# A new order for the first two batches of a fused attention and MLP kernel: v by heads, the first weight quarter in four parts, batch 1's loads held back

## The chip, the cores and the metric

The kernel runs on one core of a Trainium2 chip. The metric is the device time of one execution in microseconds (us), lower is better. Three runs of the kernel before took 324.17, 324.43 and 324.71 us; the median is 324.43. The profile is of one further execution, taken by the hardware profiler.

The engines are named as the profile names them. PE is TensorE, and PEld its weight loads. DVE is VectorE, ACT is ScalarE, POOL is GpSimd, and SP is SyncE, which here only issues DMAs.

## The reference: what is computed

There are two stages. The first is attention with a sliding window of 128 and a linear bias per head; the second is a two-layer MLP on its output.

```python
scores = scale * np.matmul(q, k.transpose(0, 1, 3, 2))      # 8 batches, 8 heads, 576 x 576, d = 64
mask = (rel >= 0) & (rel < window)                          # rel = query - key, window = 128
scores = np.where(mask, scores + bias[None], -1000000000.0) # bias = -slope[h] * |rel|
attn = softmax(scores); attn_out = attn @ v
x = attn_out.transpose(0, 2, 1, 3).reshape(4608, 512)
h = x @ w_in                                                # 512 -> 2048
g = h * np.clip(h + 3.0, 0.0, 6.0) / 6.0
out = g @ w_out                                             # 2048 -> 512
```

Inputs and output are float32; matmuls run in bf16.

## The kernel before, in words

**Attention** goes by pairs of heads: pair g is batch g // 4, heads 2(g % 4) and the next, 32 pairs in all. A query block of 128 needs only the key block on the diagonal and the one before it. For each pair PE computes the transposed scores into two PSUM tiles, `scd` (diagonal blocks, `scores_diag`) and `sco` (the blocks off it, `scores_off`). ACT takes the exponentials into bf16 tiles `pd` and `po`; in batches 1 and later POOL masks with a select (`exp_diag`, `exp_off`). In batch 0 both tiles, and in batch 1 `sco`, get bias and mask from a table that PE adds by a matmul with the identity (`tables_diag`, `tables_off`). Then PE multiplies by v, which has a column of ones so that the sum of the softmax comes along (`attend` into one tile of the score pool, `attend_split` into two half tiles of other pools, `values` in later batches). DVE takes the reciprocal and multiplies ("norm" of the pair, into `avs`, two buffers). `back` turns the result over into `xT`, by PE and a copy on ACT (on DVE for pairs 7 and part of 3) or, for most pairs from 8 on, by a transposing DMA.

**q and k** arrive in float32, are cast to bf16 (`prepare`, `prepare_double`), turned over on PE and copied to `qTb` and `kTb` (`transposes`, `double_begin` with `double_copy`, `wide_double` through a tile of the score pool, `double`). **v** arrives in token blocks of 128 (`load_block`, 256 KB each, in pieces of 256 bytes) and is cast into `vbuf` (`cast_v`, `cast_tokens`).

**The MLP** goes by blocks `nt` of 512 tokens, nine in all. An up unit U(nt, ms) is four matmuls of 512 columns into one bank `hps`, one per quarter `ks` of the model width, that is per pair of the batch; then ACT takes a relu (L516) and DVE a multiply (L517), which frees the bank. A down unit D is four of the sixteen matmuls (L547) of 128 tokens; after the fourth unit DVE copies the row out (L556). Unit U(0, ms) with ms from 4g to 4g + 3 needs column quarter g of `w_in`. The first quarter comes as plain float32 into `raw`, which lies in `gbuf[0]`, and is cast on chip (`load_raw`, `cast_raw`); the other three are casting DMAs that POOL issues (`load_w_in`), and so is `w_out` in four parts (`load_w_out`). `w_out`'s buffer holds batch 0's `pd` and `po` before, and `gbuf[1]` those of batch 1.

**Order.** The order on every engine is the order of the program (manual scheduling); an engine that waits holds all that stands behind it. `units` lists all U and D, by the strings in `ORDER`; `fill(n)` emits the next n units, but stops at a U whose tokens are not yet finished (`done`). `first_batch` and `second_batch` write the first two batches out by hand, then `segment` runs pairs 8 to 31, with `FILLS` units at fixed places of each pair.

**PSUM.** There are eight banks: two tiles of two banks for scores ("sc"), one "av", two "h", one "o". `hps` takes "h"; for nt = 0 `UP_BANKS` sends units 2, 8, 12 to "av" and 5, 11 to "o". A down row takes "o", except the first of nt = 1 and two of the last block.

**Queues.** SP issues nearly all loads, in order; ACT issues the first k loads and one v block. Plain DMAs share eight completion semaphores in turn, so that one can be issued only when the one eight before it has landed. POOL's casting DMAs stand in POOL's own order among its casts and selects.

The lines that the change and the prediction touch: `load_block` L108, `memsets` L140 and `memsets_later` L144, `load_raw` L176, `cast_raw` L179, `second_w_in` L187, `cast_v` L191, `prepare_double` L235, `wide_double` L276, `exp_diag` L371, `attend_split` L444, `back` L462, `up_begin` L496, `ORDER` L559, `first_batch` L604, `second_batch` L679, `FILLS` L741.

Of the kernel before, what the change touches and what calls it, by code (L numbers as in the profile page):

```python
# [10 lines left out]
FP32 = mybir.dt.float32  # L11
# [7 lines left out]
def kernel(  # L19
# [120 lines left out]
    def memsets():  # L140
        nc.gpsimd.memset(vbuf[0][:, :, :, D:W], 1.0)
        nc.gpsimd.memset(vbuf[0][64:128, 4, :, 0:D], 0.0)

    def memsets_later():  # L144
        for i in range(2):
            nc.gpsimd.memset(p4buf[i], 1.0)
        nc.gpsimd.memset(kTb[1][:, :, 4, LAST:128], 0.0)
        nc.gpsimd.memset(vbuf[1][:, :, :, D:W], 1.0)
        nc.gpsimd.memset(vbuf[1][64:128, 4, :, 0:D], 0.0)
        nc.gpsimd.memset(tbuf[64:128, :, 4, :], 0.0)  # L150
# [310 lines left out]

    def back(g, tag=None):  # L462
        b, hp = divmod(g, NP)
# [6 lines left out]
        tag = tag or ("o" if b < 2 else "h")  # L470
        tp = BANKS[tag].tile([128, SP], BF16, tag=tag, name="tb", padded_shape=[128, 1024])
        for j in range(NQ):
# [22 lines left out]

    def up_begin(nt, ms, n):  # L496
        hps = ps_h.tile([128, NT], FP32, tag="h", name="hps")
        up_mms(nt, ms, 0, n, hps)
        begun[nt, ms] = hps, n
# [34 lines left out]
    def moe_down(nt, step):  # L534
# [14 lines left out]
        if part == 3:  # L549
# [36 lines left out]
    def stage_next(g):  # L586
# [14 lines left out]
        if VCAST.get(g):  # L601
            cast_tokens(VCAST[g], "v")

    def first_batch():  # L604
        prepare(0, (V, A))
        load_block(0, "v", 1, nc.scalar)
        for j in (4, 0, 2, 3):
            load_block(0, "v", j, nc.sync)
        load_raw()
        warm_up(5)  # L610
        tables_diag(0)
        tables_off(0)
# [12 lines left out]
        exp_full(1)  # L625
        double_copy(0, 1, "q", 0, (V, V))
        double_copy(0, 1, "k", 0, (A, A))
        scores_diag(2)
        double_copy(0, 1, "q", 1, (V, V))
        double_copy(0, 1, "k", 1, (V, V))  # L630
        tables_off(2)
        scores_off(2)
        exp_full(2)
        scores_diag(3)
        cast_v(0, 4, P)
        cast_v(0, 0, P)
        cast_v(0, 1, P)
        cast_v(0, 2, V)
        cast_v(0, 3, V)
        scores_off(3)  # L640
        exp_full(3)
        attend(0)
        for dp in range(2):
            for nm in "kq":
                load_double(1, dp, nm, nc.sync)
        load_tokens(1, "v")
        attend_split(1, ("av", "h"))
        attend(2)
        back(0, "o")
        cast_raw(0, P)  # L650
        cast_raw(1, P)
        attend(3)
        cast_raw(2, A)
        back(1, "av")
        cast_raw(3, P)
        prepare_double(1, 0, (P,), "k")
        second_w_in()
        up_begin(0, 0, 1)
        up_begin(0, 1, 1)
        back(2, "o")  # L660
        prepare_double(1, 0, (V,), "q")
        up_more(0, 0, 2)
        up_more(0, 1, 2)
        back(3, "av")
        wide_double(1, 0, "k", V)
        wide_double(1, 0, "q", A)
        up_more(0, 0, 3)
        up_more(0, 1, 3)
        done[0] = NP
        fill(2)  # L670
        prepare_double(1, 1, (P,), "k")
        load_w_in(2)
        prepare_double(1, 1, (P,), "q")
        load_w_in(3)
        for dp in range(2):
            for nm in "kq":
                load_double(2, dp, nm, nc.sync)

    def second_batch():  # L679
        scores_diag(NP + 0)  # L680
        exp_diag(NP + 0, 0)
        exp_diag(NP + 0, 1)
        fill(2)
        scores_off(NP + 0)
        exp_off_full(NP + 0)
        wide_double(1, 1, "k", V)
        fill(1)
        wide_double(1, 1, "q", V)
        fill(1)
        scores_diag(NP + 1)  # L690
        exp_diag(NP + 1, 0)
        exp_diag(NP + 1, 1)
        fill(2)
        scores_off(NP + 1)
        exp_off_full(NP + 1)
        fill(1)
        cast_tokens(1, "v")
        scores_diag(NP + 2)
        exp_diag(NP + 2, 0)
        exp_diag(NP + 2, 1)  # L700
        fill(1)
        scores_off(NP + 2)
        exp_off_full(NP + 2)
        fill(2)
        for i in range(0, 4):
            load_w_out(i)
        g = 2 * NP - 1
        scores(g)
        exp_diag(g, 0)
        exp_diag(g, 1)  # L710
        prepare_double(2, 0, (V, P))
        prepare_double(2, 1, (P, P))
# [5 lines left out]
        exp_off_full(g)  # L718
        fill(1)
        attend(NP)  # L720
        fill(1)
        attend(NP + 1)
        fill(1)
        back(NP)
        attend(NP + 2)
        fill(1)
        back(NP + 1)
        double(2, 0, "k", 0, "av", A)
        attend(NP + 3)
        back(NP + 2)  # L730
        double(2, 0, "k", 1, "av", A)
        wide_double(2, 0, "q", A)
        up_begin(1, 0, 3)
        back(2 * NP - 1)
        up_begin(1, 1, 3)
        done[0] = 2 * NP
        fill(2)
# [52 lines left out]
    with tc.manual_schedule(engines=every):  # L790
# [7 lines left out]
        memsets()  # L798
        memsets_later()
        first_batch()  # L800
        second_batch()
        fill(2)
        segment(2 * NP, G, lambda g: FILLS.get(g, (1, 1, 1, 2, 0, 1, 2)))
# [32 lines left out]
```

## Time and profile before

| | us |
|---|---|
| device time, median of three (lowest, highest) | 324.43 (324.17, 324.71) |
| profiled execution: first to last instruction (span) | 321.8 |
| PE busy in the span | 308.2 (96%) |
| ACT, DVE, POOL busy | 196.0, 175.5, 138.4 |
| bytes moved by DMA | 52.43 MB, 118977 of 131426 packets under 512 B |
| one matmul of 512 columns, start to start, at full clock | 0.216 |
| one up or down unit of four such | 0.865 |

The profiler gives the span and not a device time of its own for that execution; 324.43 less 321.8 leaves 2.6 us around the span.

How to read it: a line of the timeline has the start, the length, the engine, the line of the code, the operation, output and input tiles and their shape, and how many instructions were merged; in brackets stands how long the engine sat idle before it and what it waited for. In the chain of waits each line is a start, a length and what the time went to. The end of a matmul is modelled, so a busy PE can still wait: where it matters, starts are compared.

### The profile page before, as it was taken

The numbers are of one execution on the slowest core, as the hardware profiler recorded it, in microseconds if no ns is written. First come the engines' busy times: TensorE is split into PE (matmuls) and PEld (weight loads), VectorE is DVE, ScalarE is ACT, GpSimd is POOL, SyncE is SP. The second block draws the span as 40 slices with busy tenths as digits, with TensorE's granted clock in tenths as the row PEclk, the third lists the DMA queues.
The fourth block names the chain that finished last, engine by engine and source line by source line (L and its number), as shares of the span: only waits on it lengthen the run. The fifth ranks groups of instructions, "written<-read, shape, count | busy, mean of one in ns | idle before, by whom it ended". The sixth has DMA issues, their size and how long they took to land.

```text
span 321.8 us, 6865 instructions
## 1 busy us (share of the span) xinstructions
PE 308.2 (96%) x2620; PEld 164.6 (51%) x2659; DVE 175.5 (55%) x346; ACT 196.0 (61%) x337; POOL 138.4 (43%) x247
## 2 busy tenths in 40 slices
PE   6888999999999999999999999999999999999996
PEld 3564465455555545455667655455454444444443
DVE  6686595564346655555555556554655455445510
ACT  3857977877777766766676667666764344244401
POOL 7364590665494767446654663663331000000000
PEclk9999999999999999999999999999999999999999
DMA  7999999899999999999799999922011200000112
GB/s 273 262 369 210 269 233 214 235 200 189 201 256 170 242 200 189 204 202 230 179 214 207 211 189 202 236 66 89 20 55 59 80 34 34 33 33 35 65 49 83
DMA packets 131426, 52.43 MB, mean 163 GB/s; under 512 B 118977, under 2 KB 122817, under 8 KB 131393
## 3 DMA queue, kind: packets, MB, share of 16 engines
q1 hardware_dynamic: 125648, 46.15, 67.0%
q0 software_dynamic: 3696, 3.67, 7.0%
q10 hardware_dynamic: 2048, 2.16, 2.2%
q8 instruction: 21, 0.34, 0.5%
q14 instruction: 13, 0.10, 0.1%
HBM read 36.70 MB, written 9.44 MB: 143 GB/s over the span
## 4 chain that ended last, share of the span: by engine, by line
PE 83%; DMA 7%; ACT 4%; issue 2%; DVE 2%; POOL 1%; SPq 0%; ACTq 0%; DVEq 0%
PE ops L547 37%; PE hps L492 35%; DMA gbuf<-in_moe_w_in_dram 3%; PE scd L324 2%; DMA w_in_sb<-in_moe_w_in_dram 2%; PE av L419 2%; DMA ldbuf<-in_k_dram 2%; PE av L411 2%; ACT r L516 2%; PE sco L356 1%; PE ops L528 1%; DVE gbuf L517 1%; PE tp L254 1%; ACT gbuf L379 1%; ACT xT L479 1%
## 5 line engine op out<-in xcount | busy, mean ns | idle before, releaser
L517 DVE SCALAR_TENSOR_TENSOR gbuf<-r,hps 128x512 bf16<-128x512 f32 x144 | 98.5, 687 | 102.3 <-ACT r L516 99.4
L516 ACT ACTIVATE r<-hps,bias 128x512 f32<-128x512 f32 x144 | 98.8, 690 | 90.4 <-PE hps L492 89.3
L492 PE MATMUL hps<-xT,w_in_sb 128*128 128x512 bf16 (+1 forms) x622 | 143.3, 357 | 2.3 <-DMA w_in_sb<-in_moe_w_in_dram 0.9
L547 PE MATMUL ops<-w_out_sb,gbuf 128*128 128x512 bf16 x539 | 134.0, 379 | 2.4 <-issue 1.7
L492 PEld LDWEIGHTS <-w_in_sb 128*128 128x128 bf16 x640 | 59.0, 98 | 55.3 <-issue 1.7
L547 PEld LDWEIGHTS <-gbuf 128*128 128x128 bf16 x560 | 52.2, 98 | 56.9
L382 POOL TENSOR_SCALAR_AFFINE_SELECT pd<-pd 128x512 bf16<-128x512 bf16 x48 | 29.5, 631 | 37.8 <-ACT pd L379 37.7
L392 POOL TENSOR_SCALAR_AFFINE_SELECT po<-po 128x512 bf16<-128x512 bf16 x48 | 30.1, 633 | 32.6 <-ACT po L389 32.4
L556 DVE COPY osb<-ops 128x512 f32<-128x512 f32 x33 | 22.7, 688 | 22.0 <-PE ops L547 21.9
L379 ACT ACTIVATE pd<-scd,bias_d 128x512 bf16<-128x512 f32 x48 | 31.5, 684 | 4.7 <-PE scd L324 4.7
L389 ACT ACTIVATE po<-sco,bias_o 128x512 bf16<-128x512 f32 x48 | 33.1, 690 | 0.0
L206 POOL CAST tbuf<-ldbuf 128x512 bf16<-128x512 f32 (+1 forms) x45 | 25.5, 611 | 17.1 <-issue 17.1
L430 DVE TENSOR_TENSOR avs<-av,rc 128x384 bf16<-128x384 f32 (+1 forms) x48 | 23.6, 491 | 1.6
L419 PEld LDWEIGHTS <-pd 128*128 128x128 bf16 x192 | 14.3, 97 | 7.9 <-issue 0.5
L411 PE MATMUL av<-vbuf,po 128*128 128x65 bf16 x192 | 18.0, 193 | 0.0
L419 PE MATMUL av<-vbuf,pd 128*128 128x65 bf16 x192 | 17.3, 194 | 0.0
L411 PEld LDWEIGHTS <-po 128*128 128x128 bf16 x192 | 14.3, 98 | 2.9 <-DVE avs L430 0.5
L395 ACT ACTIVATE p4buf<-sco,bias_d 128x64 bf16<-128x64 f32 x48 | 15.6, 325 | 0.0
L199 POOL CAST vbuf<-ldbuf 128x1024 bf16<-128x1024 f32 x14 | 14.2, 1041 | 2.4 <-DMA ldbuf<-in_v_dram 2.4
L324 PEld LDWEIGHTS <-kTb 64*128 64x128 bf16 x256 | 7.3, 94 | 14.3 <-issue 10.0
L324 PE MATMUL scd<-qTb,kTb 64*128 64x128 bf16 x256 | 12.7, 219 | 1.9 <-ACT kTb L232 1.2
L239 POOL CAST pr<-ldbuf 128x576 bf16<-128x576 f32 x18 | 11.5, 671 | 2.0 <-DMA ldbuf<-in_k_dram 1.9
(107 smaller groups left out, 216.7 us busy)
## 6 DMA issues: line engine op xcount, KB each, us to landing
out_dram<-osb SPq DMA_DIRECT2D x33, 256.0 KB, 2.5
ldbuf<-in_v_dram SPq DMA_DIRECT2D x31, 256.0 KB, 5.0
ldbuf<-in_q_dram SPq DMA_DIRECT2D x20, 256.0 KB, 4.8
ldbuf<-in_k_dram SPq DMA_DIRECT2D x16, 256.0 KB, 4.6
ldbuf<-in_q_dram SPq DMA_DIRECT2D x12, 288.0 KB, 6.4
ldbuf<-in_k_dram SPq DMA_DIRECT2D x12, 288.0 KB, 6.7
w_out_sb<-in_moe_w_out_dram POOLq DMA_DIRECT2D x4, 512.0 KB, 10.0
w_in_sb<-in_moe_w_in_dram POOLq DMA_DIRECT2D x3, 512.0 KB, 8.6
```

The source lines that it names most:

```text
L206: nc.gpsimd.tensor_copy(out=tbuf[:m, :, j, :], in_=s[:m, j, :, :].rearrange("p (i e) d -> p i (e d)", e=2))
L324: nc.tensor.matmul(scd[:, e, ts(j, 128)], lhsT=kT[r, j, :], rhs=qT[r, j, :], start=first, stop=first or j == 3)
L379: nc.scalar.activation(out=pd[:, e, :, :].rearrange("p j c -> p (j c)"), in_=sc[:, e, :], func=ACT.Exp, bias=bias_d[:, h:h + 1], scale=scale)
L382: nc.gpsimd.affine_select(out=pd[:, e, :, :], in_=pd[:, e, :, :], pattern=[[0, 4], [1, 128]], channel_multiplier=-1, base=0, compare_op=AL ...
L389: nc.scalar.activation(out=po[:, e, :, :].rearrange("p j c -> p (j c)"), in_=sc[:, e, :], func=ACT.Exp, bias=bias_o[:, h:h + 1], scale=scale)
L392: nc.gpsimd.affine_select(out=po[:, e, :, :], in_=po[:, e, :, :], pattern=[[0, 4], [-1, 128]], channel_multiplier=1, base=-1, compare_op=A ...
L411: nc.tensor.matmul(out_av, lhsT=po[:, e, qt % 4, :], rhs=vb[:, qt - 1, h, :], start=True, stop=False)
L419: nc.tensor.matmul(out_av, lhsT=d, rhs=vb[:, qt, h, :], start=(qt == 0), stop=True)
L492: nc.tensor.matmul(hps[:, lo:hi], lhsT=w_in_sb[:, ks, ts(ms, 128)], rhs=xT[:, ks, ds(src, hi - lo)], start=(ks == 0), stop=(ks == n_ks - 1))
L516: nc.scalar.activation(out=r6, in_=hps, func=ACT.Relu, bias=bias3[:, 0:1], scale=1.0 / 6.0)
L517: nc.vector.scalar_tensor_tensor(out=gts[nt][:, ms, :], in0=r6, scalar=1.0, in1=hps, op0=ALU.min, op1=ALU.mult)
L547: nc.tensor.matmul(ops[nt, sub], lhsT=gts[nt][:, ms, ts(sub, 128)], rhs=w_out_sb[:, ms, :], start=(ms == 0), stop=(ms == n_ms - 1))
```

## The change

- The v blocks of batch 0 are loaded by pairs of heads (`load_heads`, two DMAs of 128 KB for the first four token blocks) plus token block 4, all by SP, in the order heads 0, block 4, heads 1, heads 2, raw 0, raw 1, heads 3, raw 2, raw 3. They wait for a POOL memset that stands behind `prepare(1)`. The casts by heads (`cast_heads`) and all four casts of the raw quarter go to POOL; before, DVE cast two v blocks and ACT one raw part.
- The first w_in quarter comes in four DMAs instead of one.
- `second_w_in` goes, with its memset that waited for pair 1; `load_w_in(1)` and `load_w_in(2)` stand in `first_batch` between POOL's casts, `load_w_in(3)` behind batch 1's first k cast.
- Batch 1's first k and q loads wait for a DVE memset (`hold`) behind the norm of pair 2; the rest of batch 1's loads wait for one behind five up units.
- Pairs 0 and 1 go by `attend_split`, pair 0's between scores 2 and 3; the tables of pair 2 come ahead of its scores; `back` and `up_begin` use other banks.
- Ten units of nt = 0 come ahead of batch 1's first scores, in place of two; the values of pairs 4 and 5 come ahead of batch 1's second k and q and of pair 6. w_out's loads stand later.
- For nt = 1 the first ten units are all U, in one run behind batch 1; `FILLS` for pairs 9 to 11 has one unit less.
- Three memsets move from `memsets_later` to `memsets`, and `memsets_later` moves behind `first_batch`.

The diff, cut to its core:

```diff
+    def load_heads(b, nm, hp, eng):
+        for e in range(2):
+            h = 2 * hp + e
+            eng.dma_start(out=tokens(b, nm)[:, 0:4, h, :],
+                          in_=src_of[nm][b, h, 0:512, :].rearrange("(j p) d -> p j d", p=128))
...
-    def load_raw():
-        nc.sync.dma_start(out=raw, in_=moe_w_in[:, 0:512].rearrange("(k p) f -> p k f", p=128))
+    def load_raw(ks):
+        nc.sync.dma_start(out=raw[:, ks, :], in_=moe_w_in[ds(ks * 128, 128), 0:512])
...
-    def second_w_in():
-        nc.gpsimd.memset(w_out_sb[:, 4, 0:1], 0.0)
-        load_w_in(1)
+    def cast_heads(b, hp, copy):
+        copy(out=vbuf[b % 2][:, 0:4, ds(2 * hp, 2), 0:D], in_=ld[b, "v"][:, 0:4, ds(2 * hp, 2), :])
...
-    ORDER = [("UUDUDUUDUUD", "UUDUDUDUD", "UDUDUDD", "UDDDD"),
+    ORDER = [("UUUUUUUUUU", "UUDUDUDUD", "DUDDDDDD", "DDDDD"),
...
+    def hold(buf, col):
+        nc.vector.memset(ldbuf[buf][:, col:col + 1], 0.0)
     def first_batch():
         prepare(0, (V, A))
-        load_block(0, "v", 1, nc.scalar)
-        for j in (4, 0, 2, 3):
-            load_block(0, "v", j, nc.sync)
-        load_raw()
...
         prepare(1, (P, V))
+        nc.gpsimd.memset(ldbuf[2][:, 0:1], 0.0)
+        load_heads(0, "v", 0, nc.sync)
+        load_block(0, "v", 4, nc.sync)
+        load_heads(0, "v", 1, nc.sync)
+        load_heads(0, "v", 2, nc.sync)
+        load_raw(0)
+        load_raw(1)
+        load_heads(0, "v", 3, nc.sync)
+        load_raw(2)
+        load_raw(3)
...
         exp_full(2)
+        cast_heads(0, 0, P)
+        cast_v(0, 4, P)
+        cast_heads(0, 1, P)
+        cast_heads(0, 2, P)
+        load_w_in(1)
+        cast_heads(0, 3, P)
+        for ks in range(n_ks):
+            cast_raw(ks, P)
+        load_w_in(2)
+        attend_split(0, ("av", "o"))
         scores_diag(3)
+        attend_split(1, ("h", "h"))
         scores_off(3)
         exp_full(3)
         attend(2)
+        hold(1, 0)
+        for nm in "kq":
+            load_double(1, 0, nm, nc.sync)
+        back(0, "av")
+        back(1, "o")
         attend(3)
+        back(2, "h")
+        up_begin(0, 0, 2)
         back(3, "av")
+        up_begin(0, 1, 2, "o")
...
+    def second_batch():
+        memsets_later()
+        fill(5)
+        hold(3, 0)
+        load_heads(1, "v", 0, nc.sync)
+        load_block(1, "v", 4, nc.sync)
+        load_heads(1, "v", 1, nc.sync)
+        for nm in "kq":
+            load_double(1, 1, nm, nc.sync)
+        for hp in (2, 3):
+            load_heads(1, "v", hp, nc.sync)
         fill(2)
+        prepare_double(1, 0, (P, V), "kq")
         load_w_in(3)
+        fill(1)
+        wide_double(1, 0, "k", V)
+        wide_double(1, 0, "q", A)
...
         fill(2)
+        g = NP
+        scores_diag(g)
         exp_diag(g, 0)
         exp_diag(g, 1)
+        fill(1)
+        scores_off(g)
+        exp_off_full(g)
+        scores_diag(g + 1)
+        exp_diag(g + 1, 0)
+        exp_diag(g + 1, 1)
+        fill(1)
+        scores_off(g + 1)
+        exp_off_full(g + 1)
+        cast_heads(1, 0, P)
+        cast_v(1, 4, P)
+        cast_heads(1, 1, P)
+        fill(1)
+        attend(g)
+        fill(1)
+        attend(g + 1)
+        back(g, "o")
+        fill(1)
+        prepare_double(1, 1, (P, V), "kq")
+        back(g + 1, "o")
+        wide_double(1, 1, "k", V)
+        wide_double(1, 1, "q", A)
...
+        fill(1)
+        scores_diag(g + 2)
+        exp_diag(g + 2, 0)
+        exp_diag(g + 2, 1)
+        load_w_out(0)
+        up_begin(1, 0, 2)
+        scores_off(g + 2)
+        exp_off_full(g + 2)
+        up_begin(1, 1, 2)
+        scores(g + 3)
+        exp_diag(g + 3, 0)
+        exp_diag(g + 3, 1)
+        exp_off_full(g + 3)
+        cast_heads(1, 2, P)
+        cast_heads(1, 3, P)
+        load_w_out(1)
+        prepare_double(2, 0, (P, P), "kq")
+        load_w_out(2)
+        load_w_out(3)
+        attend(g + 2)
+        attend(g + 3)
+        prepare_double(2, 1, (P, P), "kq")
...
+        back(g + 2)
+        up_more(1, 0, 3)
+        up_more(1, 1, 3)
+        back(g + 3)
+        done[0] = 2 * NP
+        fill(4)
+        double(2, 0, "k", 0, "av", A)
         fill(1)
+        double(2, 0, "k", 1, "av", A)
         fill(1)
+        wide_double(2, 0, "q", V)
+        fill(4)
         scores_diag(2 * NP)
         scores_off(2 * NP)
 
-    FILLS = {g: (1, 1, 1, 2, 0, 1, 1) for g in range(9, 15)}
+    FILLS = {g: (1, 1, 1, 1 if g < 12 else 2, 0, 1, 1) for g in range(9, 15)}
```

More of the change, by code (lines that the diff above doesn't have):

```diff
@@ L142, in memsets @@
         nc.gpsimd.memset(vbuf[0][64:128, 4, :, 0:D], 0.0)
+        nc.gpsimd.memset(kTb[1][:, :, 4, LAST:128], 0.0)
+        nc.gpsimd.memset(vbuf[1][:, :, :, D:W], 1.0)
+        nc.gpsimd.memset(vbuf[1][64:128, 4, :, 0:D], 0.0)
     def memsets_later():
@@ L460, in by_xbar, with back @@
         return g >= XB and g not in (XB + 2, XB + 3)
-    def back(g, tag=None):
+    def back(g, tag=None, place=None):
         b, hp = divmod(g, NP)
@@ L470, in back @@
         tag = tag or ("o" if b < 2 else "h")
-        tp = BANKS[tag].tile([128, SP], BF16, tag=tag, name="tb", padded_shape=[128, 1024])
+        tp = place
+        if tp is None:
+            tp = BANKS[tag].tile([128, SP], BF16, tag=tag, name="tb", padded_shape=[128, 1024])
         for j in range(NQ):
@@ L494, in up_mms, with up_begin @@
                                  start=(ks == 0), stop=(ks == n_ks - 1))
-    def up_begin(nt, ms, n):
-        hps = ps_h.tile([128, NT], FP32, tag="h", name="hps")
+    def up_begin(nt, ms, n, tag="h"):
+        hps = BANKS[tag].tile([128, NT], FP32, tag=tag, name="hps")
         up_mms(nt, ms, 0, n, hps)
@@ L627, in first_batch @@
         double_copy(0, 1, "k", 0, (A, A))
+        tables_diag(2)
+        tables_off(2)
         scores_diag(2)
@@ L674, in first_batch @@
         load_w_in(3)
-        for dp in range(2):
+        fill(1)
+        wide_double(1, 0, "k", V)
+        wide_double(1, 0, "q", A)
+        for dp in range(1):
             for nm in "kq":
                 load_double(2, dp, nm, nc.sync)
[L679 to L682, printed above, removed]
         fill(2)
[L684 to L708, printed above, removed]
+        g = NP
@@ new lines, in second_batch @@
+        attend(g + 1)
[5 more added lines that the diff above has]
+        wide_double(1, 1, "q", A)
+        for nm in "kq":
+            load_double(2, 1, nm, nc.sync)
+        fill(1)
[7 more added lines that the diff above has]
+        up_begin(1, 1, 2)
@@ L717, in second_batch @@
         load_tokens(3, "q")
-        exp_off_full(g)
+        back(g + 2)
[5 more added lines that the diff above has]
+        double(2, 0, "k", 0, "av", A)
         fill(1)
-        attend(NP)
+        double(2, 0, "k", 1, "av", A)
         fill(1)
[L722 to L737, printed above, removed]
+        wide_double(2, 0, "q", V)
+        fill(4)
         scores_diag(2 * NP)
         scores_off(2 * NP)
-    FILLS = {g: (1, 1, 1, 2, 0, 1, 1) for g in range(9, 15)}
+    FILLS = {g: (1, 1, 1, 1 if g < 12 else 2, 0, 1, 1) for g in range(9, 15)}
     def segment(lo, hi, fills):
@@ L798 @@
         memsets()
-        memsets_later()
         first_batch()
         second_batch()
-        fill(2)
         segment(2 * NP, G, lambda g: FILLS.get(g, (1, 1, 1, 2, 0, 1, 2)))
```

36 lines of the change are left out of this document (removed).

## The prediction

> **What bounds the kernel now.** I read the busy totals first, then the busy time in four stretches of my choosing, then PE's timeline for its waits, then the chain of waits for who ends them.
>
> ```profile
> PE 308.2 (96%) x2620; PEld 164.6 (51%) x2659; DVE 175.5 (55%) x346; ACT 196.0 (61%) x337; POOL 138.4 (43%) x247
> ```
>
> PE is busy nearly all of the span, so only its waits can be won or lost. The stretches (length, then busy time of PE, PEld, DVE, ACT and POOL) say where those are:
>
> ```profile
> 0.00:24.40 24.40, 19.66 (x308) 12.01 (x309) 18.09 (x57) 14.78 (x20) 14.63 (x35) 1.00 1.05 301
> 24.40:51.20 26.80, 24.75 (x275) 14.30 (x280) 18.46 (x30) 22.65 (x35) 16.57 (x26) 1.00 1.16 234
> 51.20:92.30 41.10, 39.93 (x361) 21.04 (x366) 20.46 (x39) 29.54 (x54) 23.17 (x39) 1.00 1.07 215
> 92.30:321.80 229.50, 223.90 (x1678) 117.23 (x1704) 118.50 (x221) 129.01 (x229) 84.05 (x149) 1.00 0.64 131
> ```
>
> The stretches end where up units 0 and 1 are done (24.4), where batch 1 is done but for the last quarters of units (1,0) and (1,1) (51.2), and at unit (2,0) (92.3). In the second ACT is busy 22.65 of 26.80: little slack.
>
> Both kernels issue the same matmuls. By the strings and fills, both have emitted 52 units when unit (2,0) comes, and from there the same program. So **the change is the difference in when (2,0) runs**, that is, in PE's waits before it.
>
> I count work by starts, since ends are modelled: in the chain twelve matmuls L547 take 2.59 us, 0.216 each, 0.865 a unit. By starts in PE's timeline, batch 1's scores cost 1.2 a pair (later ones 0.56), `attend` 0.56, `back` 0.28, `wide_double` 0.50, values 0.55. From 24.4 to 51.2: 14 units 12.1, scores 4.8, attends 2.2, backs 1.1, transposes 2.0, begun units 1.3, in all 23.6, so 3.2 of waits. From 51.2 to 92.3: 34 units 29.4, rest of two 0.4, scores 3.4, values 2.2, backs 0.6, transposes 2.0, in all 38.0: 3.1 of waits. **Old waits after 24.4: 6.3.** The largest single one is the last line here:
>
> ```profile
> 21.69 0.45 PE L473 MATMUL tb<-ident,avs 128*128 128x128 bf16 x5 [0.39 <-DVE avs L441]
> ...
> 24.90 0.40 PE L324 MATMUL scd<-qTb,kTb 64*128 64x128 bf16 x8 [0.34 <-ACT qTb L284]
> ...
> 29.52 1.04 PE L492 MATMUL hps<-xT,w_in_sb 128*128 128x512 bf16 x3 [0.90 <-DMA w_in_sb<-in_moe_w_in_dram]
> ```
>
> **Part 1, batch 0: a gain of 1.3 to 2.4.** ACT's exponentials carry this part (0.92 to 1.0 each, the last ending at 17.2), and they stay; the tables of pair 2 ahead fill a wait of PE that ACT has anyway. `attend_split(0)` (18 matmuls, 0.03 apart) before scores 3 moves the last exponential some 0.3 back. Nine v DMAs in place of five and four raw in place of one cost SP 0.65 each: 13 from 6.8 (behind POOL's cast of pair 1) end at 15.2. The bytes start where they did, behind q's second quarter (lands 9.4). Before, v ended at 16.3 and raw at 19.0, at 0.68 per raw part; now two raw parts go ahead of heads 3, which so land at about 18.0 and raw at 19.4. POOL casts heads 3 (0.61) by 18.7, `attend(3)` starts at 18.75 (before 18.63), and raw's casts (0.58 each, now all on POOL) end at 21.0. Units 0 and 1 close at 22.1. The old ones close at 24.4, but with the two `wide_double` done, so 23.4 by the same work: 1.3. If the late raw and v were as even as the first v blocks (one 128 KB part every 0.67), it is 2.4. I take 1.8. The second quarter of w_in is issued at about 16; before, issue to landing was 7.5, so 23.5, where unit 4 wants it at 22.8 to 23.9: bounds 0 and 0.7, I take 0. The hold on DVE opens at 18.2, after SP is free at 15.2, so it does bind; batch 1's four loads land 0.75 apart from about 22 to 24.5, and POOL (third quarter's issue, moved memsets 1.26) casts k from 23 on: hidden by units 2 to 7, 0.6 worse without them. The memsets moved forward replace others on POOL: nothing.
>
> **Part 2, q of pairs 4, 5: a loss of 1.5.** A multiply ends 1.45 after PE has left its unit (PE leaves at 54.04; ACT 54.07, DVE 54.79 to 55.48). The q casts now stand on DVE behind unit 6's multiply:
>
> ```profile
> 41.09 1.40 DVE L239 CAST pr<-ldbuf 128x576 bf16<-128x576 f32 x2
> ```
>
> So q is ready 2.85 after unit 6; PE has unit 7 (0.865) and k's transposes (0.50) meanwhile, then nothing. At most 1.5, at least 0.5 if DVE were a unit ahead; I take 1.5.
>
> **Part 3, units 8 to 15 among batch 1's four pairs: waits of 7.5 instead of 3.2.** Before, 14 units lay in this stretch, now 8, against the same exponentials: per pair ACT needs 2.06 (starts 0.57, 0.57, 0.92 apart).
>
> ```profile
> 40.35 1.26 ACT L379 ACTIVATE gbuf<-scd,bias_d 128x512 bf16<-128x512 f32 x2
> 41.49 1.03 ACT L363 ACTIVATE gbuf<-sco 128x1024 bf16<-128x1024 f32 x1
> ```
>
> I laid out the four engines in program order by these rows, zero at unit 8. PE's waits:
> - `attend(4)`: its v casts stand on POOL behind pair 5's two selects; exponentials end 6.3, select 6.9, two casts of 0.61: 8.1. PE is there at 6.9: 1.2, and 0.15 before it on ACT.
> - `back(5)` behind norm 5: 0.8. Before, pairs had a unit more between values and `back`, and still:
>
> ```profile
> 43.13 0.69 DVE gbuf L517
> 43.82 0.14 DVE rcw L440
> 43.98 0.83 DVE avs L441
> 44.82 0.04 issue
> 44.86 0.45 PE tb L473 x5
> ```
>
>   The norm stands behind a unit's multiply; `attend(4)` had ended at 42.29.
> - second q transposes, as in part 2 behind a multiply and two casts: 1.2. Scores 6 and 7 on the copy and on ACT: 0.75.
> - `attend(6)`: its cast stands on POOL behind pair 7's selects, at 20.9; PE is there at 19.4: 1.6.
> - norm 6, copy, the begun units, norm 7's copy, with no unit between: 0.55, 0.7, 0.55.
>
> Together 7.5. Lower bound 3.2, the old stretch; no reason gives less with 6 units fewer.
>
> **Part 4, ten U in a run: a loss of 2.9.** They share the two "h" banks. A bank's turn is in the chain:
>
> ```profile
> 54.07 0.70 ACT r L516
> 54.79 0.70 DVE gbuf L517
> 55.49 0.04 issue
> 55.53 0.38 PE hps L492
> ```
>
> With PE's 0.865 before it that is 2.36; two banks give 1.18 a unit instead of 0.865. Ten units, the third waiting 1.3 for the first's bank, with 1.0 of transposes between that fill some of it: 2.9. At least 1.7: eight and a half units at 0.315 more, less those transposes. [...]
>
> **Part 5, pairs 8 to 12: waits of 2.6 against 3.1.** The fills give 8, 6, 6, 6 and 0 units, before 8, 7, 7, 7 and 3. With none for pair 12, its exponentials (87.00 to 89.84 before) and the copy after them pace it: 4.1 for 2.3 of work, 1.8. D in a row share one "o" bank (DVE copy 0.69 each four units): 0.8, bounds 0 and 2.7. w_out, issued 10 us later, is wanted only here.
>
> **Sum.** -1.8 + 1.5 + 7.5 + 2.9 + 2.6 - 6.3 = +6.4. On the profiled execution: span 321.8 + 6.4 = 328.2, with the 2.6 around it **330.8**; the runs' median 324.43 stands to it by just that 2.6. Low ends (2.4 gained; 0.5, 3.2, 1.7, 1.8): -2.4 + 7.2 - 6.3 = -1.5, 322.9. High ends (1.3, 0.7; 1.5, 7.5, 2.9, 4.5): +9.5, 333.9.
>
> **Rivals.**
> - **Smaller loss**, 325.2 to 328: the waits on POOL's and DVE's order partly cover each other. For: idle time there (DVE busy 18.46 of 26.80). Half of part 3's excess gone gives 328.6, all of it 326.5, half of part 4 too 325.0.
> - **Faster**, 322.3. One mechanism: the engines behind PE work ahead of it. With ten units before any exponential of batch 1, ACT, DVE and POOL enter the pairs with nothing queued; then the casts behind selects and multiplies cost nothing, and in part 4 the next unit finds its bank free. That takes 1.2, 0.8, 1.2 and 1.6 from part 3, 0.8 from part 5 and 2.9 from part 4: 1.5 + 2.7 + 0 + 1.8 - 1.8 - 6.3 = -2.1. It decides once the new waits after unit 4 fall below 8.1; I count 14.5. For it: the 0.90 for w_in goes, and ACT needs 0.58 a unit to PE's 0.865. Against: ACT's 22.65 of 26.80, and the bank's turn of 2.36 holds with nothing queued.
> - **A late transfer**, 335.6: heads 3 or w_in's second quarter come 3 us later, as raw's parts and POOL's DMAs now share the engines, and PE's clock falls meanwhile. PE's first matmuls ran at half rate (512 columns in 0.43) from 1.4 to 5.1, 3.7 us that lose 1.8: 330.8 + 3 + 1.8. For it: issue to landing of w_in varied from 7.5 to 10.3. Against: both have a microsecond or so, and a wait of 1.2 at 6 us left 0.216 as it was. [...]
> - **No change**, 324.4: the holds don't bind and the reordered waits come out alike. Against: the first hold binds by 3 us, and parts 2 to 4 name waits of their own.
>
> **Chances.** Forecast (328 to 334) 0.66; smaller loss 0.15; faster 0.10; within 0.2% (about what a measurement can tell here) 0.03; late transfer 0.06. Slower so 0.87. The range 325.5 to 334.5 leaves out the faster case, no change, and the ends of two others.
>
> **What would show it.** Part 1: units 0, 1 done at 21 to 22.1. Part 2: about 1.5 idle at the second L282 group, released by DVE L239. Part 3: PE waiting at L419 for POOL casts by heads. Part 4: L492 starts 1.18 a unit apart, released by L517. Part 5: unit (2,0) near 98.7. Wrong, if PE's waits from unit 4 to (2,0) sum below 8.

## The result, and the profile after

The changed kernel takes 340.99 us (median of 4 runs, 340.78 to 341.44) beside 324.30 (323.97 to 324.71) for the kernel before in the same session: a ratio of 1.0523 [1.0508, 1.0539], 16.7 us slower. Forecast were 330.8, in a range that ended at 334.5. The sign was right; the loss is 2.6 times the forecast one (6.4). Of the runs below one, e1's of 343.6 us, fell into a slower state and is left out.

These are rows of the page of the kernel after: busy times (share of the span, instructions), then PE's busy tenths in 40 slices of 8.5 us, and the granted clock in the same slices. The span is 339.1.

```profile
PE 318.1 (94%) x2659; PEld 167.7 (49%) x2659; DVE 175.6 (52%) x348; ACT 196.3 (58%) x336; POOL 139.9 (41%) x252
PE   7997875979997999999999999999999999999996
PEclk9999997699999999999999999999999999999999
```

DVE, ACT and POOL are as busy as before (175.5, 196.0, 138.4): nothing was added for them to do. PE's row is thin in most slices from the fourth to the ninth, 25 to 76 us, and once more in the thirteenth (pair 12); in the seventh and eighth the clock is below full.

The stretches after stand at marks by the same work as before: units 0 and 1 done (22.34), unit 8 starts (30.53), the last quarter of unit (1,0) (57.33), scores of pair 8 (71.71), the last quarter of unit (2,0) (109.13; before 92.33). Columns as before: length, busy PE, PEld, DVE, ACT, POOL, then granted clock, DMA share, GB/s.

```profile
22.34:30.53 8.19, 6.49 (x44) 3.34 (x43) 6.60 (x12) 5.26 (x8) 2.53 (x4) 1.00 1.05 214
30.53:57.33 26.80, 19.89 (x239) 11.51 (x237) 13.60 (x22) 17.52 (x25) 14.24 (x24) 0.96 0.93 227
57.33:71.71 14.38, 12.25 (x52) 5.24 (x52) 6.55 (x9) 7.20 (x11) 2.51 (x5) 0.72 1.02 188
71.71:109.13 37.42, 33.22 (x334) 18.14 (x334) 15.38 (x31) 24.01 (x45) 22.08 (x37) 1.00 0.88 172
```

PE's work in the last three, counted by starts as in the prediction, is 17.4, 8.35 (eight units, one half of a unit, 18 transposes) and 30.7. The waits are the rest: 9.4, 6.0 and 6.7. With 1.9 in the first stretch, less the 6.3 of old waits and the 1.1 gained ahead of 22.34, that is +16.6, and (2,0) is 16.8 later. From there to the end it is 230.0 against 229.5, so everything of importance lies ahead of (2,0), as the prediction had it.

PE's timeline after, its starts with the longer idle times (in brackets: idle before, released by):

```profile
30.01 0.68 PE L288 MATMUL tp<-ident,pr 128*128 128x128 bf16 x9 [1.70 <-DVE pr L245]
...
45.03 0.68 PE L288 MATMUL tp<-ident,pr 128*128 128x128 bf16 x9 [1.65 <-DVE pr L245]
...
52.17 0.23 PE L425 MATMUL wide<-vbuf,gbuf 128*128 128x65 bf16 x2 [1.51 <-POOL vbuf L199]
...
59.48 3.57 PE L500 MATMUL hps<-xT,w_in_sb 128*128 128x512 bf16 x8 [1.14 <-DVE gbuf L525]
...
75.08 1.02 PE L500 MATMUL hps<-xT,w_in_sb 128*128 128x512 bf16 x4 [1.27 <-DVE gbuf L525]
...
83.87 1.02 PE L555 MATMUL ops<-w_out_sb,gbuf 128*128 128x512 bf16 x4 [0.56 <-DVE osb L564]
...
106.01 0.20 PE L417 MATMUL av<-vbuf,po 128*128 128x65 bf16 x1 [0.88 <-DVE avs L436]
...
107.62 0.20 PE L356 MATMUL sco<-qTb,kTb 64*128 64x64 bf16 x2 [0.86 <-ACT p4buf L401]
```

The first three rows are waits that parts 2 and 3 named: both q transposes behind DVE's casts (L245), `attend(6)` behind POOL's cast by heads (L199); `attend(4)`, left out here, waits 0.53 for the same. The next, at 59.48, is the "h" banks of part 4 (another such wait, at 69.89, is 0.84). The ten U of part 4 are all behind PE when the scores of pair 8 start at 71.71, so the wait at 75.08 is not theirs: it is the second U of pair 8, unit (1,11). One of the two "h" banks holds half of k's transposes there (`double`), and the other is freed by the multiply of unit (1,10). Then comes the "o" bank of part 5, once more with 0.54 at 94.86. The last two are in pair 12; the prediction priced that pair as a whole (1.8) and named neither. Eight matmuls that take 3.57 at 59.48 run at half rate (at 69.89 eight take 1.89): that is the clock.

### The profile page after: what moved, and what is told of

The parts are those of the page before. It is cut to its first block, busy times and chain, and to the rows that moved or that the text cites. A ratio compares the mean times of both kernels' runs of the same rounds, so it can differ in the third digit from the quotient of the medians.

```text
span 339.1 us, 6923 instructions
## 1 busy us (share of the span) xinstructions
PE 318.1 (94%) x2659; PEld 167.7 (49%) x2659; DVE 175.6 (52%) x348; ACT 196.3 (58%) x336; POOL 139.9 (41%) x252
## 4 chain that ended last, share of the span: by engine, by line
PE 85%; ACT 6%; DVE 4%; DMA 2%; issue 2%; POOL 0%; SPq 0%; DVEq 0%; POOLq 0%; ACTq 0%
PE ops L555 36%; PE hps L500 33%; PE scd L330 3%; DMA ldbuf<-in_q_dram 2%; PE av L425 2%; PE av L417 2%; PE sco L362 2%; ACT r L524 2%; DVE gbuf L525 1%; PE ops L536 1%; PE scd L305 1%; PE tp L260 1%; ACT gbuf L385 1%; ACT xT L487 1%; PE w L163 1%
## 5 line engine op out<-in xcount | busy, mean ns | idle before, releaser
L500 PE MATMUL hps<-xT,w_in_sb 128*128 128x512 bf16 (+1 forms) x640 | 147.9, 364 | 4.8 <-DVE gbuf L525 3.3
L555 PE MATMUL ops<-w_out_sb,gbuf 128*128 128x512 bf16 x560 | 137.8, 379 | 1.1 <-DVE osb L564 1.1
L500 PEld LDWEIGHTS <-w_in_sb 128*128 128x128 bf16 x640 | 60.0, 99 | 61.4 <-issue 9.6
L398 POOL TENSOR_SCALAR_AFFINE_SELECT po<-po 128x512 bf16<-128x512 bf16 x48 | 30.1, 632 | 31.4 <-ACT po L395 31.1
L212 POOL CAST tbuf<-ldbuf 128x512 bf16<-128x512 f32 (+1 forms) x45 | 25.5, 611 | 16.6 <-issue 11.8
L245 POOL CAST pr<-ldbuf 128x576 bf16<-128x576 f32 x18 | 11.5, 667 | 4.7 <-DMA ldbuf<-in_k_dram 2.4
L205 POOL CAST vbuf<-ldbuf 128x1024 bf16<-128x1024 f32 x12 | 12.1, 1040 | 0.0
```

What stands on the lines that cost most here:

```text
L212: nc.gpsimd.tensor_copy(out=tbuf[:m, :, j, :], in_=s[:m, j, :, :].rearrange("p (i e) d -> p i (e d)", e=2))
L398: nc.gpsimd.affine_select(out=po[:, e, :, :], in_=po[:, e, :, :], pattern=[[0, 4], [-1, 128]], channel_multiplier=1, base=-1, compare_op=A ...
L500: nc.tensor.matmul(hps[:, lo:hi], lhsT=w_in_sb[:, ks, ts(ms, 128)], rhs=xT[:, ks, ds(src, hi - lo)], start=(ks == 0), stop=(ks == n_ks - 1))
L555: nc.tensor.matmul(ops[nt, sub], lhsT=gts[nt][:, ms, ts(sub, 128)], rhs=w_out_sb[:, ms, :], start=(ms == 0), stop=(ms == n_ms - 1))
```

## Experiments

Three theories stood after the result. **Clock**: PE's lower clock from 55.1 us costs the unforeseen part. **Order**: the forecast's mechanisms hold and were under-priced, in the run of U and in pairs 8 to 12 above all. **Casts**: the waits on POOL's and DVE's queue order in part 3 are the core, and take the rest with them. Where no other kernel is named, a kernel is the changed one with one edit; +x is its median less that of the kernel before in the same session (323.86 for the first four, 324.41 for the next four, 324.19 for the last two).

### e1_busy_waits: idle waits filled with useless matmuls

```
         load_w_out(3)
+        warm_up(7)
         attend(g + 2)
...
         back(g + 2)
+        warm_up(4)
         up_more(1, 0, 3)
...
-        fill(4)
+        warm_up(3)
+        fill(2)
+        warm_up(5)
+        fill(2)
```

> The changed kernel with 19 spare matmuls of 512 columns put into four of PE's waits (7 before the values of pair 6, 4 before the begun units' third quarter, 3 and 5 around the first two units of the run); their result is not used. In the changed kernel's profile the granted clock is 0.5 from 55.1 to 65.3. Theory (the half clock has a price of its own, set off by PE's waits between 50 and 57): the clock stays at 1.0 there, matmuls of 512 columns start 0.216 apart instead of 0.43, and the time falls by 3 to 4, to about 337.5. Rival (the clock falls where PE waits anyway, so it costs nothing): within 0.7 of 341.0. A second rival (the low clock comes from the start or from power, not from waits): the clock falls all the same.

Measured: 338.35 (337.37 to 339.36, three runs), 1.0444 [1.038, 1.0507], +14.5. These runs differ by their mean granted clock, 1.0 in the quickest and 0.99 in the longest. The profiled one has the clock at 1.0 throughout from 6.2 us on, and so shows the change without the clock:

```profile
29.98:56.13 26.15, 22.02 (x254) 12.42 (x251) 13.62 (x22) 17.53 (x25) 13.60 (x23) 1.00 0.92 220
56.13:68.03 11.90, 10.29 (x58) 4.76 (x57) 6.55 (x9) 7.21 (x11) 3.21 (x6) 1.00 1.04 178
```

Against the rows of after: 0.65 less in the first, 2.5 in the second; the third, up to the last quarter of (2,0) at 105.44, is at 37.41 beside 37.42. The clock so explains 3.1 of the 10 us that were missed (the two profiled spans, 339.1 and 335.7, differ by 3.4), and 13.1 of lateness at (2,0) remain (105.44 less 92.33). The clock theory holds for a third of the gap at most.

With the clock up the chain of waits of the run can be read (start, length, what):

```profile
56.54 0.70 ACT r L524
...
57.33 0.70 DVE gbuf L525
...
58.08 1.04 PE hps L500 x4
...
62.24 0.72 ACT kTb L262
...
64.30 1.27 DVE qTb L290
65.57 0.60 DVE gbuf L525
```

The bank's turn is as priced, relu, multiply, next matmul. But between relu and relu stands a copy of the k transposes (0.72 on ACT), and between multiply and multiply the copy of the q transposes (1.27 on DVE). The prediction let these transposes fill 1.0 us of PE's waits and forgot that their copies, 2.0 us together, stand in the queues of the two engines that free the bank. So the run waits 3.55 here (11.90 less 8.35 of work; PE's useless matmuls lie in these waits), where 2.9 were forecast.

### e2_early_casts: the casts of heads 2 and 3 before pair 7's selects

```
         prepare_double(1, 1, (P, V), "kq")
+        cast_heads(1, 2, P)
+        cast_heads(1, 3, P)
...
-        cast_heads(1, 2, P)
-        cast_heads(1, 3, P)
         load_w_out(1)
```

> The changed kernel with the casts of v heads 2 and 3 of batch 1 put on POOL right behind batch 1's second k cast instead of behind pair 7's selects. Theory (POOL's order makes PE wait 1.6 before the values of pair 6, and that wait helps to lower the clock): the wait of 1.5 at 52.2 falls to under 0.3; by itself 1.3 less, and if the clock then stays up 3 more: 336.5 to 339.7. Rival (the transfer of heads 2, 3 or the exponentials hold the values anyway): within 0.5 of 341.0.

Measured: 339.22 (337.18 to 340.8), 1.0451 [1.039, 1.0513], +15.4. PE's timeline has at `attend(6)`, in place of the 1.51 that POOL's cast ended,

```profile
50.52 0.22 PE L425 MATMUL wide<-vbuf,gbuf 128*128 128x65 bf16 x2 [0.23 <-ACT gbuf L385]
```

and from unit 8 to the last quarter of (1,0) it takes 24.86 us instead of 26.80. So the queue order on POOL costs what part 3 said (1.6), and no more: the casts theory takes the rest along with nothing. The medians show only 1.3 of the 1.9, within their spread; in the profiled run the clock was low for 3.4 us at 56.2 and again at 104.0.

### e3_four_banks: the run of U on four PSUM banks

```
+    UP_BANKS_1 = {2: "o", 5: "o", 6: "av", 9: "o"}
...
-            tag = UP_BANKS.get(ms, "h") if nt == 0 else "h"
+            tag = {0: UP_BANKS, 1: UP_BANKS_1}.get(nt, {}).get(ms, "h")
```

> The changed kernel with units 2, 5, 9 of the ten U in the o bank and 6 in the av bank, so that the run rotates over four banks instead of two. Theory of the prediction (two banks cost 2.9 in this run): 2 to 3 less, 338 to 339. Rival (the clock is at half there, a unit takes 1.71 of PE, more than a bank's turn of 2.36 over two, so banks bind only at the first units and after 65): 0.5 to 1.5 less, about 340.

Measured: 337.48 (337.02 to 338.32), 1.0404 [1.0362, 1.0446], +13.6. The run:

```profile
57.63:68.04 10.41, 10.13 (x54) 4.62 (x53) 6.41 (x9) 6.97 (x11) 2.27 (x5) 0.85 1.12 193
```

The run takes 10.41 instead of 14.38, with the same matmuls in it, and of the 2.06 left above 8.35 some 1.5 is the clock (at 0.5 until 60.7, so half of 3.07). In the kernel after the clock cost this run 2.5, so about 1.0 of the 3.97 saved is the clock and 3.0 the banks. PE has no wait for a multiply in it any more. The bank's turn is what made the run slow. Nothing moves in pairs 8 to 12: 37.41 here, 37.41 in e1, 37.42 after. They lose on their own account, and unit (1,11) waits as before (the multiply is L526 in this kernel):

```profile
71.41 1.02 PE L500 MATMUL hps<-xT,w_in_sb 128*128 128x512 bf16 x4 [1.27 <-DVE gbuf L526]
```

### e4_old_order: the old ORDER string under the changed fills

```
-    ORDER = [("UUUUUUUUUU", "UUDUDUDUD", "DUDDDDDD", "DDDDD"),
+    ORDER = [("UUDUDUUDUUD", "UUDUDUDUD", "UDUDUDD", "UDDDD"),
```

> The changed kernel with the order string of the kernel before for the second block (U and D mixed from its third unit on) in place of ten U first. Fills stay as changed. Theory (the run of U costs 2.9 by its banks, and rows of D alone in pairs 9 to 11 cost another 1 to 2 by the single o bank): 2.5 to 4.5 less, 336.5 to 338.5. Rival (w_out's parts, which land at 54.9 to 65.4, are then waited for by the first D): within 1 of 341.0, with PE waiting for a DMA into w_out_sb before L555.

Measured: 335.63 (334.98 to 337.15), 1.0351 [1.0304, 1.0398], +11.8, so the new order costs 4.9 of the 16.7 here. The run is at 10.33, as with four banks, since every D between two U gives the banks time (PE waits once for a multiply there, 0.27), and pairs 8 to 12 take 35.89 instead of 37.42.

### e5_spread: units kept back for pair 12

```
-    FILLS = {g: (1, 1, 1, 1 if g < 12 else 2, 0, 1, 1) for g in range(9, 15)}
+    FILLS = {g: (1, 1, 1, 0 if g < 12 else 2, 0, 1, 1) for g in range(9, 15)}
```

> The changed kernel with five units each in pairs 9 to 11 instead of six, so that pair 12 gets three; nothing else. In the changed kernel pair 12 runs from its scores at 104.1 to the last quarter of unit (2,0) at 109.1, 5.0 for 2.3 of PE's work, while in the kernel before it had three units. Theory (pair 12 is paced by ACT's exponentials and PE idles there for want of units): the three units fill that idle time, 2.0 to 2.6 less, about 338.6. Rival (the units taken from pairs 9 to 11 hid waits of their own, at the o bank and behind values): within 0.7 of 341.0.

Measured: 339.95 (339.85 to 340.07), 1.0459 [1.0402, 1.0517], +15.5. Pairs 8 to 12 take 36.12 instead of 37.42.

The run is 1.2 less than after, between the rival's 0.7 and the theory's 2.0. Three units beside pair 12's exponentials take 1.3 off, less than the two waits that they were to cover (0.88 and 0.86 in the timeline after, 1.05 and 1.04 by starts): a new wait of 0.42 for the "o" bank's copy appears at 90.12, since D still stand in a row there.

### e6_v_alone: in the kernel before, part 1 alone

Here the base is the kernel before: v by heads and the first quarter of w_in in four parts, without the holds, the fills and the order.

```
-        load_block(0, "v", 1, nc.scalar)
-        for j in (4, 0, 2, 3):
-            load_block(0, "v", j, nc.sync)
-        load_raw()
+        load_heads(0, "v", 0, nc.sync)
+        load_block(0, "v", 4, nc.sync)
+        for hp in (1, 2, 3):
+            load_heads(0, "v", hp, nc.sync)
+        for ks in range(n_ks):
+            load_raw(ks)
...
+        cast_heads(0, 0, P)
         cast_v(0, 4, P)
-        cast_v(0, 0, P)
-        cast_v(0, 1, P)
-        cast_v(0, 2, V)
-        cast_v(0, 3, V)
+        cast_heads(0, 1, P)
+        cast_heads(0, 2, V)
+        cast_heads(0, 3, V)
```

> The kernel before with one part of the change alone: batch 0's v by heads and the first w_in quarter in four plain parts, all by SP in the order heads 0, block 4, heads 1 to 3, raw 0 to 3; casts by heads on POOL (two on DVE, as before). Theory (batch 0 is paced by ACT's exponentials, and the bytes are the same): within 0.5 of the kernel before. Rival, the prediction's first part (the load order is worth 1.3 to 2.4 by itself): 1 or more faster than the kernel before. A second rival (eight more DMAs on SP push batch 1's k and q back): 0.5 to 1.5 slower, with PE waiting at the transposes of batch 1.

Measured: 325.86 (325.03 to 327.04, 10 runs), 1.004 [1.0015, 1.0065], +1.4: a small loss. PE's timeline shows where the earlier start goes:

```profile
22.50 0.68 PE L291 MATMUL tp<-ident,pr 128*128 128x128 bf16 x9 [0.64 <-POOL w_out_sb L194]
...
24.66 0.68 PE L291 MATMUL tp<-ident,pr 128*128 128x128 bf16 x9 [1.47 <-DVE pr L248]
```

That is the second rival. The last `back` of batch 0 starts 0.28 sooner (21.41, before 21.69); then PE waits at batch 1's transposes for POOL's k casts, which end at 22.45, and for DVE's q casts, which had waited 1.81 for q's load. In the kernel before the same q casts started at 21.55 without a wait. The clock is at 0.5 for 3.4 us from 25.3. In the changed kernel units 0 and 1 close 1.1 to 1.3 sooner, with five units ahead of these transposes; but there other edits help (pair 0's values ahead of scores 3, all raw casts on POOL, batch 1's loads held back), so how much of that gain is the load order's was not separated.

### e7_q_on_pool: both q casts on POOL

```
-        prepare_double(1, 1, (P, V), "kq")
+        prepare_double(1, 1, (P, P), "kq")
```

> The changed kernel with the second q casts of batch 1 on POOL behind the k casts instead of on DVE behind a unit's multiply and norm 5. In the changed kernel PE waits 1.8 between the two groups of transposes at 43.2. Theory (DVE's order makes that wait): it falls under 0.3, 1.2 to 1.8 less by itself, and the half clock later gets shorter or goes: 336.5 to 339.7. Rival (norm 5 and the copies that follow pace this stretch): the wait moves to the scores of pair 6, within 0.5 of 341.0.

Measured: 339.80 (339.27 to 341.54), 1.0463 [1.0406, 1.0521], +15.4. The wait at the second q transposes is gone, but in the profiled run the first q waits twice as long:

```profile
31.39 1.14 PE L288 MATMUL tp<-ident,pr 128*128 128x128 bf16 x9 [3.12 <-DVE pr L245]
```

Its casts (29.0 and 30.6) themselves waited 1.5 us for q's load, and the clock fell at 31.1. The stretch behind unit 8 gains 0.45 alone, because units 8 and 9 run at half clock there: 2.92 (32.32 to 35.24) instead of 1.82 (30.53 to 32.35). Without that it would gain 1.55, near the 1.8 by starts of the wait that went. The profiled run, 341.54, is the slowest of the four: there a load that nothing in the edit concerns takes all of the gain. This run can't separate the two; e8 can.

### e8_combined: old order, early casts, q on POOL, units kept back

The edits of e4, e2, e7 and e5 together.

> The changed kernel with four of its own edits undone or moved together: the old order string for the second block, v casts of heads 2 and 3 behind the second q casts, these on POOL, and three units left for pair 12. By the single runs so far: about 5 for the order, 1.5 to 2 for the casts, 1.5 for q, 2 for pair 12, some of it the half clock that then should not come: 328 to 332. If this beats the kernel before (324), the holds and the load order were worth having; if it stays slower, ten units ahead of batch 1 leave too few units beside its exponentials, which the prediction's third part says.

Measured: 331.96 (331.33 to 332.04), 1.0209 [1.0161, 1.0256], +7.6, with the clock at 1.0 in the profiled run:

```profile
30.06:53.08 23.02, 19.18 (x239) 11.23 (x237) 12.28 (x20) 17.52 (x25) 14.72 (x24) 1.00 0.99 241
...
63.99:100.29 36.30, 33.57 (x334) 17.64 (x334) 16.85 (x34) 26.05 (x48) 23.14 (x39) 1.00 0.89 206
```

The stretch between them takes 10.91. The waits are 5.6, 2.6 and 5.6, in all 13.8 (and 1.6 at the first q) beside the 6.3 before. The first stretch is 1.84 shorter than in e2, which has the early casts alone: that is the second q's wait, here without a low clock. The waits on POOL's cast at `attend(6)`, on DVE's casts at the second q and on pair 12's scores and values are gone; but waits of 0.89 and 1.22 on the norm's bank now stand at the second group of values in pairs 9 and 10, and 1.24 of the second stretch is a D that waits for w_out's load. What these edits don't give back are the units that the changed kernel spends ahead of unit 8, which before lay beside the exponentials of batch 1 and of pairs 8 to 12. That these units are what is missing is argued: no run kept them back. Over half of the loss is mended, and the kernel before is still ahead.

### e10_order_in_old: in the kernel before, the new ORDER alone

```
-    ORDER = [("UUDUDUUDUUD", "UUDUDUDUD", "UDUDUDD", "UDDDD"),
+    ORDER = [("UUUUUUUUUU", "UUDUDUDUD", "DUDDDDDD", "DDDDD"),
```

> The kernel before with the new ORDER string alone; loads, casts and FILLS are those of before. Theory (the new order costs by its ten U in two banks and by the units that pairs 8 to 12 then lack, with or without the clock): the run takes 2 to 3 us more and pairs 8 to 12 about 1.5 us more, so 327 to 329 us with the granted clock at 1.0 throughout. Rival (the order is dear only where PE's work has been thinned out before it and the clock falls): within 1 us of the kernel before, 324 to 325.5 us. If the run alone is enough to bring the clock down, 330 us or more and a stretch of 0.5 in the clock's row.

Measured: 330.5 (329.96 to 330.67), 1.019 [1.0169, 1.021], +6.3, more than the theory's own 3 to 5 and with the clock at 1.0 throughout. From scores 8 to scores 9, first the kernel before,

```profile
51.58:61.97 10.39, 10.07 (x68) 4.84 (x69) 5.42 (x9) 7.70 (x14) 3.35 (x6) 1.00 1.02 218
```

then this one:

```profile
52.65:67.84 15.19, 10.91 (x67) 4.92 (x69) 8.03 (x12) 10.53 (x18) 4.49 (x7) 1.00 1.06 237
```

Both rows hold ten units and pair 8's scores and transposes, 9.7 of work, so this kernel waits 5.5 where the one before waits 0.7. From scores 9 to (2,0) it takes 31.56 against 30.36, with the same 24 units in both: 1.2 more of waits. The remaining 1.1 of the 7.1 that (2,0) is later in the profiled run is ahead of pair 8, where the two kernels are the same program. The chain of waits shows a bank's turn made longer by pair 8's exponentials, which stand between the relus on ACT:

```profile
60.83 0.68 ACT pd L379
61.51 0.59 ACT r L516
...
62.12 0.70 DVE gbuf L517
```

So a run of U on two banks is dear wherever it is put, and the new order as a whole costs 6.3 in the kernel before and 4.9 in the changed one.

### e9b_half_exps: e8 with half of batch 1's diagonal exponentials

```
+        m = 2 if full(g) else 4
-        nc.scalar.activation(out=pd[:, e, :, :].rearrange("p j c -> p (j c)"),
-                             in_=sc[:, e, :], func=ACT.Exp,
+        nc.scalar.activation(out=pd[:, e, 0:m, :].rearrange("p j c -> p (j c)"),
+                             in_=sc[:, e, 0:m * 128], func=ACT.Exp,
...
-                    d = pd[:, e, qt, :]
+                    d = pd[:, e, qt % 2 if full(g) and not diag_tabled(g) else qt, :]
```

> The combined kernel (old order, early casts, q on POOL, units spread), with the diagonal exponentials and selects of pairs 4 to 7 on 256 of their 512 columns; the values of these pairs use the first two diagonal tiles twice, so two of four diagonal tiles are left out. It takes 8 x about 0.28 us off ACT and 8 x about 0.2 us off POOL between unit 8 and the last quarter of batch 1. Theory (what is left there, 5.6 us of PE's waits, is PE having no units to put beside the chain scores, exponentials, select, values of one pair): the chain of each of four pairs gets some 0.5 to 1 us shorter, the stretch 23.0 to 20 or 21 us, so 329 to 330 us. Rival (the waits are for casts and landings, which this leaves as they are): the stretch stays at 22.5 to 23.0 us and the time at 331.5 to 332 us.

Measured: 330.95 (330.32 to 331.07), 1.0205 [1.0187, 1.0223], +6.8. The stretch behind unit 8:

```profile
30.58:52.66 22.08, 18.52 (x235) 11.13 (x237) 12.38 (x20) 16.05 (x25) 13.44 (x25) 1.00 0.95 245
```

It is 0.94 shorter, where the theory wanted 2 to 3 and the rival at most 0.5: neither. ACT was given 1.5 and POOL 1.3 less to do, and PE got two thirds of it. So the exponentials pace a part of these 5.6 us only; PE's timeline still has the waits on the norms and copies (0.60, 0.27, 0.73 and 0.55), which this leaves as they are. That units beside the pairs would cover all of it is argued from the kernel before, not shown by this run.

## Why the prediction was right on the sign and wrong on the size

By its own terms, with e1 as the profile without the clock. Part 4 is the run of ten U up to scores 8, part 5 what lies between scores 8 and (2,0), 26 units in both the prediction and the kernel.

| term | predicted | after | e1 |
|---|---|---|---|
| part 1, batch 0 | -1.8 | -1.1 | -1.3 |
| part 2, first q | +1.5 | +1.9 | +1.6 |
| part 3, unit 8 to (1,0) | +7.5 | +9.4 | +8.75 |
| part 4, ten U | +2.9 | +6.0 | +3.55 |
| part 5, pairs 8 to 12 | +2.6 | +6.7 | +6.7 |
| old waits | -6.3 | -6.3 | -6.3 |
| sum | +6.4 | +16.6 | +13.0 |

So the prediction missed 10.2. Part 5, sized at 2.6, holds 4.1 of it; the clock, at nothing in the sum, 3.1 (0.65 in part 3, 2.5 in part 4); part 3 without the clock 1.25, part 4 without it 0.65; parts 1 and 2 together 1.1.

**Part 1** was right in kind, 0.5 to 0.7 too large. Units 0 and 1 close at 22.34, just behind the 21 to 22.1 that were named, and in e6, where the load order stands without the rest, nothing of it reaches the end: PE meets batch 1's k and q too early.

**Part 2** was right: by starts 1.57 to 1.58 in e1 to e5 and e8. In the profile after, the second half of q lands as late as 29.2 (the prediction had 24.5), and DVE waits another 0.2 for it.

**Part 3** was right in its mechanism, with each wait that was named present: 0.53 and 1.51 for POOL's casts, 1.65 for the second q, the norms and copies behind. e2 removes one of them and gains what it was said to cost. Of the 1.9 that it is off by, 0.65 is the clock; the rest is mostly the second q (1.8 by starts, forecast 1.2) and the last three waits, on norm 6 and the two copies (2.5, forecast 1.8).

**Part 4** was near without the clock, 2.9 against 3.55, and far with it, 6.0. The 0.65 is the sentence in which the transposes between the units "fill some of it": they do on PE, but their copies, 0.72 on ACT and 1.27 on DVE, stand in the bank's turn. The turn itself, 2.36, was near (2.52 in e1, from 58.08 to 60.60). e3 shows the mechanism from one side (four banks, run at 10.4), e10 from the other (the run alone in the old kernel, waits of 5.5 with the clock up). For these ten units two banks were too few and four were enough: in e3 PE waits for no multiply in the run, and 3.0 of the 3.97 saved are the banks. The upper end of part 4 in the range was the estimate itself, with no room above, and so was part 3's: that, an upper end of 4.5 in part 5, and no clock in the sum are why the range ended too early.

**Part 5 is the step that failed**, 2.6 against 6.7, with the clock at 1.0 all through it. Pair 12 takes 5.0 (104.1 to 109.1) for 2.3 of work: 2.7, not 1.8. The prediction priced its exponentials, but not that in a pair without units the scores of pair 13 (0.86, on ACT's p4) and the second group of values (0.88, on the norm's bank) each wait by themselves. Unit (1,11) waits 1.4 by starts (1.27 in the timeline) for an "h" bank; the prediction counted the sharing of these banks only in part 4, and here k's transposes share them too. The "o" bank cost 1.4 instead of 0.8, within its bounds; 1.2 is spread over small gaps, which the prediction put at nothing. e5 takes 1.3 off by units for pair 12, e4 1.5 by the old order string.

**The clock** appeared only in a rival, at a chance of 0.06, and tied to a late transfer. It fell without one. Its size in that rival was 1.8, and 3.1 was measured; that the forecast's own waits might bring it down was not weighed (in e1, with matmuls in four of them, the profiled run's mean clock was 1.0).

**The rivals.** The faster one priced the casts and banks at nothing because the engines would be ahead; the timeline has all of them. "Smaller loss" supposed that waits cover each other; they added up instead, as PE meets them one after another in its own order. The test that was set, PE's waits from unit 4 to (2,0) below 8, came out at 24.0 (1.9 + 9.4 + 6.0 + 6.7).

## What to carry to other kernels

Units of plain matmuls are worth most, as this case suggests, beside the stretches where another engine sets the pace; spent earlier, they gained little here and left each later wait bare. When matmul groups share two banks, list all that stands in the queues of the engines that empty the banks, copies of transposes and exponentials too, and every other tile that takes one of these banks, and not only the two instructions of the turn. And when a count finds many small waits close together, give the sum an upper end above itself, and ask what the clock does there (here it cost 3.1 us).

## What the runs showed of the hardware that was not expected

In the kernel after the granted clock fell to 0.5 at 55.10 with no wait of PE above 1.51 us in the 9 us before. It was low until 65.34, that is 10.24 us; these are stretches of the kernel after, each as long as a third of that; the seventh column, behind the five busy times, is the clock:

```profile
41.40:44.81 3.41, 1.71 (x18) 0.92 (x16) 2.78 (x5) 1.89 (x3) 0.00 (x0) 1.00 0.98 312
...
51.69:55.10 3.41, 1.73 (x41) 1.49 (x41) 2.00 (x4) 0.62 (x2) 3.41 (x6) 1.00 0.99 156
55.10:58.51 3.41, 2.56 (x9) 1.08 (x9) 0.46 (x1) 0.64 (x2) 3.41 (x6) 0.50 1.06 163
```

In the stretch before the fall PE is busy 1.73 of 3.41. In e6, where the clock fell at 25.3, PE is busy 1.32 of the 3.40 us before; in e7 the first fall, at 31.1, lay in a wait of 3.12. But in the first row here PE is busy 1.71, no more than before the fall, and the clock stays at 1.00. So the busy share alone doesn't decide it, and what does is open. Low stretches lasted 3.4 us in e2 and e6, 6.8 in e3 and e4, 10.2 after and in e5. A low stretch of 10.2 us cost 3.1 us here, since PE waited through part of it anyway.

A load that the edit doesn't touch moved by several microseconds: batch 1's q, behind a hold, was forecast at 24.5 and had its second half at 29.2 in the profile after. In e7 the same load held PE's wait at 3.12 instead of 1.70, which undid much of the edit's gain.
